# One set of block-diagonal input rows, late modulations side by side, one parameter chain moved to GpSimd, in an adaLN + S4D convolution + token MLP kernel

## The chip, the core and the metric

The kernel runs on one core of a Trainium2 chip. The metric is the device time of one execution in microseconds; the time of a kernel is the median of its runs. The engines are named as in the profile: PE (TensorE), PEld (its weight loads), DVE (VectorE), ACT (ScalarE), POOL (GpSimd) and SP (SyncE, which here only issues DMAs).

## What is computed

The input u has 2048 tokens of 448 channels. Six modulation vectors come from `silu(c) @ w_mod`. They are called 0 to 5 below, in the order of this code. Cut to what matters:

```python
sa, ca, ga, sb, cb, gb = split(silu(c) @ w_mod)       # modulations 0..5, 448 each
h = layernorm(u) * (1 + ca) + sa
# S4D: per channel d a kernel K[d, l] from 256 complex modes, l < 2048
K = 2 * Re(sum_n C[d,n] dt[d] * exp(A[d,n] dt[d] * l))
y = irfft(rfft(h, 4096) * rfft(K, 4096))[:2048] + h * D_skip
x = u + ga * y
h = layernorm(x) * (1 + cb) + sb
out = x + gb * (W2 gelu(W1 h^T + b1) + b2)^T           # along the tokens, F = 1792
```

## The kernel before

Most of the first half is the making of K. The 448 channels are taken in 28 groups of 16, each in two halves, which gives 56 steps, numbered s. For a step PE multiplies small tables with the parameters of its channels (`st_exponents`, `st_phase`: tiles xe and xg in PSUM), ACT takes exponentials and sines, POOL multiplies the magnitudes with the sines (G, two products, L649 and L650) and makes the magnitudes of the upper half (w, m: L628, L630, `st_mag2`), DVE makes E from PSUM (four products, L651 to L655, with two operands of which one is in PSUM), and PE contracts E with G (`st_kgen`, tile kg). Exponentials and sines lie in different table sets of ACT, so the exponentials of eight steps are taken together: `window(s)` at s = 0, 8, 16, ... holds 16 exponentials (L612, tile mag) with their table products, and after it the eight steps have only sines, six ACT instructions each. In a step all engines take their part in an order that is fixed by the code; `flush(dve)` and `flush(act)` put queued closures on those engines. PE, DVE, ACT and POOL each work in program order. The order of the DMAs on SP is set by a scheduler while the pool `first` is open, and is program order from where `first.close()` stands, which is at s = 8.

The parameters of the 448 channels are prepared in four sets of at most 128 channels ("chains", q = 0 to 3). `first_chain` does set 0 ahead of step 0. `chain(q)` does the others a few operations at a time: eight operations on DVE and ACT, then logarithms and exponentials on ACT inside `logs` at the start of window 8, 16 or 24, then 28 more on DVE (tiles of 128 by 256: s, ph, u, xa, p64 and their split into two parts hl, which a DMA on SP stores to `pars`). `WPACE` says how many of these go behind each of the eight exponentials of a window, `pace` how many into each step. `load(g)` reads `pars` back as lex and lph, the operands of the table products.

Beside this runs the input side. `x_load` brings the tokens (tile xt, 16 rows r of 128 tokens by 448), `u_stats` takes mean and variance (L492, L493), `u_scale` the scale and shift, `u_norm` applies them (L508 on ACT, L510 on POOL). Then the first pass of the Fourier transform over the tokens, "rows": `u_rows` multiplies 32-token blocks with the table WU (L523: pu in PSUM), DVE scales by mod[1] on the way out (L526: yt), SP stores yu_d. The second pass, "columns": `u_load` reads yu_d transposed (yi), `u_cols` multiplies with the table S2 (L555), DVE or ACT copies out (L562, L564: uo; DVE where the mod[0] term with the table SV is added), SP stores us_d. The PSUM tiles of rows, columns and modulations come from one pool of three buffers. The rows run in windows 8 and 16 and in steps 8 to 15, the columns in window 24 and in steps 17 to 31. The `modulation` products take the 112 by 448 blocks of w_mod with a broadcast silu(c) (L479: pm, all 128 rows equal), and ACT copies to mod[k] (L483). Number 1, 2 and 3 are made in steps 2 to 7, number 0 at the start of window 8, numbers 4 and 5 at the start of window 16; the last two are loaded into xt.

From step 32 on the products of the two spectra (second channels' half and inverse transform) run under the steps, until about 432 us; then the token MLP: two large products of PE with weights split into two parts by ACT and DVE.

Of the kernel before, what the change touches and what calls it, by code (L numbers as in the profile page):

```python
# [22 lines left out]
P = 128  # L23
# [8 lines left out]
DC = 224  # L32
# [7 lines left out]
def dft_tables():  # L40
# [16 lines left out]
    t["WU"] = np.tile(w1.transpose(1, 2, 0).reshape(32, 64), (4, 1))  # L57
# [45 lines left out]
    t["S2"] = su.reshape(2, 4, 8, 2, 32 * P).transpose(3, 0, 2, 1, 4).reshape(P, 32 * P)  # L103
# [113 lines left out]
def tile_adaln_s4d_mixer(ctx, tc, i, out):  # L217
# [6 lines left out]
    yu_d = dram.tile([2, 32, 2, 8, 4, D], F32, name="yu_d")  # L224
    us_d = dram.tile([2, 32, P, DC], F32, name="us_d")
    v_d = dram.tile([32, P, D], F32, name="v_d")
    x2_d = dram.tile([L, D], F32, name="x2_d")

# [9 lines left out]
    with ExitStack() as es:  # L238
# [27 lines left out]
        def par_load(q):  # L266
            n = min(P, D - P * q)
            raws[q] = {}
            for nm in ("A_C_real", "A_C_imag", "A_log_A_real", "A_A_imag"):
                raws[q][nm] = qp.tile([P, N], F32, tag=nm, name=nm, bufs=2)  # L270
                nc.sync.dma_start(raws[q][nm][0:n], i[nm][P * q : P * q + n])
# [40 lines left out]
        wu = xp.tile([P, 64], F32, name="wu")  # L312
        wms = {}

        def wm_load(k, tile, eng=nc.sync):
            wms[k] = tile
            eng.dma_start(wms[k], i["w_mod"][:, k * D : (k + 1) * D].rearrange("(q p) d -> p q d", p=PP))
# [11 lines left out]
        def wm_slot(k):  # L329
            w = wm0.rearrange("p k d -> p (k d)")[0:PP]  # L330
            return w[:, 4 * D * (k % 4) : 4 * D * (k % 4 + 1)].rearrange("p (q d) -> p q d", q=4)

        late = {
            2: lambda: wm_load(2, wm_slot(2), G),
            3: lambda: wm_load(3, wm_slot(3), G),
            5: lambda: wm_load(0, wm_slot(0), G),
            6: lambda: [
# [3 lines left out]
            9: lambda: nc.sync.dma_start(svt, i["SV"]),  # L343
            10: lambda: [s2_load(0), s2_load(1)],
            11: lambda: [s2_load(2), s2_load(3)],
            12: lambda: wm_load(4, xt[0:PP, 0:4]),
            13: lambda: wm_load(5, xt[0:PP, 4:8]),
# [14 lines left out]

        def chain(q):

# [39 lines left out]
            stt(s, t, -80 * math.log(2.0) / 2.0**80, s, ALU.mult, ALU.add)  # L404
            yield
            stt(s, ya, 0.5, s, ALU.mult, ALU.add)
            yield
            ts(s, s, ldt2[0:n, q : q + 1], None, ALU.add)
# [4 lines left out]
            ts(ph, aim, dt4[0:n, q : q + 1], None, ALU.mult)  # L413
            yield
            ts(u, ph, MAGIC, MAGIC, ALU.add, ALU.subtract)
            yield
            tt(ph, ph, u, ALU.subtract)
# [3 lines left out]
            ts(u, ph, 128.0, MAGIC, ALU.mult, ALU.add)  # L421
            yield
            ts(u, u, MAGIC, None, ALU.subtract)
            yield
            stt(p64, ph, 128.0, u, ALU.mult, ALU.subtract)
# [3 lines left out]
            ts(xa, xa, 4 * i2p, -0.5, ALU.mult, ALU.add)  # L429
            yield  # L430
            ts(u, cr, 0.0, 0.5, ALU.is_ge, ALU.subtract)
            yield
            tt(xa, xa, u, ALU.mult)
            yield
            ts(u, ci, 0.0, 0.5, ALU.is_ge, ALU.subtract)
            yield
            stt(xa, xa, 0.5, u, ALU.add, ALU.mult)
            yield
            stt(xa, ph, 63.0, xa, ALU.mult, ALU.add)
            yield  # L440
            ts(u, xa, MAGIC, MAGIC, ALU.add, ALU.subtract)
            yield
            tt(xa, xa, u, ALU.subtract)
            yield
            yield from split(xa, [(2, 0)])
        def logs(root=False):

            for a, s, u, xa, ya in tmp.values():
                S.activation(u, ya, AF.Square)
                S.activation(s, s, AF.Ln)  # L450
                S.activation(u, u, AF.Ln, bias=1.0)
            if root:
                S.activation(rs, mv[:, :, 1], AF.Ln, bias=eps_t)
# [20 lines left out]
        def modulation(k, *halves):  # L474
# [887 lines left out]
```

## Time and profile before

| | us |
|---|---|
| median of 3 runs | 719.2 |
| lowest and highest run | 718.16 and 723.35 |
| the profiled execution | 723.32 |
| its span | 721.5 |
| mean granted clock of PE | 0.924 of full speed |
| PE, DVE, ACT, POOL busy | 630.4, 453.3, 442.9, 273.4 |

The profiled execution took 1.8 us more than its span, and 4.1 more than the median. A row of a group of instructions has line, engine, operation, the tile written and the tile read with the shapes, the count, busy time and mean time of one in ns, and then the idle time of the engine ahead of those instructions and what ended it. A matmul on 32-bit operands stands as two rows in the trace. The granted clock of PE is 0.50 when the clock is halved and 1.00 at full speed.

### The profile page before, as it was taken

The page shows a single profiled execution, that of the slowest core. Times are in us where ns is not written, and L with a number is a line of the kernel's source. Part 1 is how long each engine was busy: PE and PEld are TensorE (multiplying, and loading weights), DVE is VectorE, ACT ScalarE, POOL GpSimd, SP SyncE. Part 2 cuts the span into 40 slices and gives each one's busy share as a digit, 9 for nine tenths or more (in the row PEclk, how much of TensorE's full clock was granted, in tenths as well). Part 3 has the DMA queues.
Part 4 walks back from the last instruction along what each step waited for, and adds up shares of the span by engine and source line. Part 5 has one row for each costly group of instructions (what it writes and reads, how often), then busy time and mean ns, then how long its engine had stood idle before and what let it go on. Part 6 is the DMA issues. An engine that isn't in the chain of part 4 may idle for free. (4 is left out here: it accounts for less than half of the span.)

```text
span 721.5 us, 18291 instructions
## 1 busy us (share of the span) xinstructions
PE 630.4 (87%) x7204; PEld 455.2 (63%) x7204; DVE 453.3 (63%) x875; ACT 442.9 (61%) x879; POOL 273.4 (38%) x328
## 2 busy tenths in 40 slices
PE   0659989987899888789888949999999999999997
PEld 0334334543544546556565617778999999999996
DVE  7569779769859768476785538778723263334441
ACT  5837588777988889989983549787622242222220
POOL 6487428318729788878884600000000000000000
PEclk9869857787999999989999959999999999999999
DMA  7795464356889645535236979974585436655540
GB/s 168 203 192 139 147 198 138 114 186 164 245 250 254 183 137 131 162 86 152 71 105 184 289 221 257 243 207 112 167 233 153 143 106 176 175 156 153 154 141 25
DMA packets 101636, 121.19 MB, mean 168 GB/s; under 512 B 13067, under 2 KB 87423, under 8 KB 101423
## 3 DMA queue, kind: packets, MB, share of 16 engines
q1 hardware_dynamic: 100014, 113.16, 55.3%
q0 software_dynamic: 1536, 6.87, 4.4%
q8 instruction: 57, 0.93, 0.6%
q14 instruction: 29, 0.23, 0.1%
HBM read 84.64 MB, written 34.87 MB: 166 GB/s over the span
## 5 line engine op out<-in xcount | busy, mean ns | idle before, releaser
L202 ACT CAST whi<-w 128x896 fp32r<-128x896 f32 x64 | 59.7, 938 | 131.4 <-PE o L1329 84.6
L649 POOL TENSOR_TENSOR G<-mag,gs 128x512 f32<-128x512 f32 x56 | 71.9, 1283 | 92.4 <-ACT gs L645 92.4
L211 DVE TENSOR_TENSOR wlo<-w,whi 128x896 fp32r<-128x896 f32 x64 | 68.0, 1087 | 40.3 <-ACT whi L202 27.9
L601 PE MATMUL xg<-tab,lph 64*128 64x512 f32 x112 | 68.0, 609 | 26.6 <-issue 7.9
L1194 PE MATMUL acc<-h3h,whi 128*128 128x448 f32 x224 | 83.5, 373 | 0.1
L1195 PE MATMUL acc<-h3l,whi 128*128 128x448 f32 x224 | 82.0, 366 | 0.0
L1329 PE MATMUL o<-ul,whi 128*128 128x448 f32 x224 | 81.3, 363 | 0.0
L676 PEld LDWEIGHTS kg<-E,G 128*32 128x32 f32 x3584 | 60.7, 121 | 32.5 <-issue 19.4
L1328 PE MATMUL o<-uh,whi 128*128 128x448 f32 x224 | 81.2, 362 | 0.0
L1196 PE MATMUL acc<-h3h,wlo 128*128 128x448 f32 x224 | 81.1, 362 | 0.0
L1330 PE MATMUL o<-uh,wlo 128*128 128x448 f32 x224 | 80.6, 360 | 0.0
L601 PE MATMUL xe<-tab,lph 64*128 64x512 f32 x112 | 66.7, 599 | 12.2 <-ACT gs L646 10.0
L676 PE MATMUL kg<-E,G 128*32 128x64 f32 x3584 | 70.8, 237 | 3.1 <-issue 2.3
L650 POOL TENSOR_TENSOR G<-mag,gs 128x512 f32<-128x512 f32 x56 | 71.7, 1280 | 0.0
L651 DVE TENSOR_TENSOR E<-m,xe 128x512 f32<-128x512 f32 x56 | 38.2, 683 | 39.6 <-ACT xe L644 31.5
L630 POOL TENSOR_TENSOR m<-mag,w 128x512 f32<-128x512 f32 x56 | 59.9, 1069 | 6.0 <-DVE E L655 1.5
L1332 DVE SCALAR_TENSOR_TENSOR y<-o,b,mod 128x448 f32<-128x448 f32 x16 | 10.9, 684 | 80.3 <-PE o L1330 80.3
L642 ACT ACTIVATE ab<-xe 128x512 f32<-128x512 f32 x56 | 33.6, 600 | 31.0 <-PE xe L601 18.4
L1194 PEld LDWEIGHTS acc<-h3h,whi 128*128 128x128 f32 x224 | 42.4, 189 | 13.9 <-ACT h L1250 6.3
L601 PE MATMUL xe<-tab,lex 64*128 64x512 f32 x56 | 31.2, 567 | 19.2 <-DMA lex<-wm 17.4
L601 PEld LDWEIGHTS xg<-tab,lph 64*128 64x128 f32 x112 | 24.0, 214 | 37.1 <-issue 9.8
L612 ACT ACTIVATE mag<-xe 128x512 f32<-128x512 f32 x56 | 35.5, 634 | 17.8 <-PE xg L601 11.1
(231 smaller groups left out, 1485.9 us busy)
## 6 DMA issues: line engine op xcount, KB each, us to landing
w<-in_B_w_dram SPq DMA_DIRECT2D x64, 224.0 KB
w<-in_B_w_dram SPq DMA_DIRECT2D x32, 448.0 KB
yu_d<-yt SPq DMA_DIRECT2D x16, 448.0 KB
yi<-yu_d SPq DMA_DIRECT2D x32, 224.0 KB
us_d<-uo SPq DMA_DIRECT2D x16, 448.0 KB
u<-us_d SPq DMA_DIRECT2D x32, 224.0 KB
v_d<-vt SPq DMA_DIRECT2D x32, 224.0 KB
vt<-v_d SPq DMA_DIRECT2D x16, 448.0 KB
```

The lines of the kernel that those rows point to most:

```text
L211: eng.tensor_tensor(lo, w, hi.bitcast(F32), ALU.subtract)
L601: T.matmul(out[k], lhs[r], rhs[r], start=start, stop=stop)
L630: G.tensor_tensor(m2, me, w[:, :, None].to_broadcast([P, GD, 32]), ALU.mult)
L649: G.tensor_tensor(Gt[:, 1], mg_, v32(sg), ALU.mult)
L650: G.tensor_tensor(Gt[:, 0], mg_, v32(cg_), ALU.mult)
L676: T.matmul(kgs[g][32 * q : 32 * q + 32, m], Gt[:, c, d], E[:, c, d], start=h == 0 and c == 0 and m == 0, stop=h == 1 and c == 1, skip_grou ...
L1194: nc.tensor.matmul(acc[f], hi[:, fs], h3h[:, r], start=r == 0, stop=False)
L1195: nc.tensor.matmul(acc[f], hi[:, fs], h3l[:, r], start=False, stop=False)
L1196: nc.tensor.matmul(acc[f], lo[:, fs], h3h[:, r], start=False, stop=r == 15)
L1328: nc.tensor.matmul(o, hi[:, ks], uh[kh][:, k], start=kh == 0 and k == 0, stop=False)
L1329: nc.tensor.matmul(o, hi[:, ks], ul[kh][:, k], start=False, stop=False)
L1330: nc.tensor.matmul(o, lo[:, ks], uh[kh][:, k], start=False, stop=kh == 1 and k == 6)
```

## The change

It has seven parts.

1. *Rows.* WU becomes block-diagonal: 128 by 128, two blocks of 32 tokens beside each other, so a product takes 64 rows of tokens and gives 128 rows, where it took 32 and gave 64. `u_rows(r)` now does one row of 128 tokens with two products (before: 32 calls with two products each). All 16 rows go into window 8, two behind each of the exponentials 1 to 5 and three behind 6 and 7; of the last ones three rows' products and six yt come in step 8. The layouts of yu_d and S2 follow.
2. *Norms.* Rows 0 to 3 are scaled on DVE, the other twelve on ACT in window 8 (before six on POOL, ten on ACT, eight of these in steps 8 to 15).
3. *Columns.* They begin in step 10 (before in step 17), one or two a step, three each in windows 16 and 24; us_d is stored in 32 pieces of 224 KB instead of 16 of 448 KB. `u_load` begins in step 9 (before 16).
4. *Modulations.* Only 1, 2 and 0 are made early, in steps 2 to 7. Numbers 3 to 5 are made together in steps 19 to 22 by twelve narrow products (32 equal rows each, three side by side in one PSUM tile), copied by ACT as one row each, stored to mod_d in DRAM and read back broadcast. The one that is added to 1 is finished on POOL at step 26. The product of mod[0] and mod[2] moves from DVE in window 8 to POOL in step 8.
5. *Second channels' chain.* The 28 later operations of chain(1) go to POOL, all in window 8, with their six stores on POOL's DMA queue; operations of three inputs become two instructions (`fuse`). The eight earlier ones go from steps 0 to 4 into window 0, and the loads of its parameters onto ACT's queue in `first_chain`. The later operations of the chains 2 and 3 stay on DVE, and lie fully in windows 16 and 24, the earlier ones one per step.
6. *SP.* `first.close()` moves from s = 8 to s = 16, and the SP order up to there becomes program order: the early loads of SV and S2 are issued at steps 9 and 10. The first four rows of u are loaded by SP behind the first lph loads (before by POOL). `u_stats` moves to steps 1 to 7. The loads of a group that begins a new set are issued two steps later.
7. *Tables.* `logs` names the set that holds both logarithm and exponential ahead of its first instruction.

The core of the diff:

```diff
-    t["WU"] = np.tile(w1.transpose(1, 2, 0).reshape(32, 64), (4, 1))
+    wu = np.zeros((2, 2, 32, 32, 2, 2))
+    for g in range(2):
+        wu[:, g, :, :, :, g] = w1.transpose(1, 2, 0)
+    t["WU"] = wu.reshape(P, P)
...
+        def fuse(eng, out, a, c, b, op0, op1):
+            if eng is V:
+                stt(out, a, c, b, op0, op1)
+                return
+            part = a if out is b else out
+            eng.tensor_scalar(part, a, c, None, op0)
+            eng.tensor_tensor(out, part, b, op1)
+
         def chain(q):
+            late_eng = G if q == 1 else V
...
-                V.tensor_copy(hl[:, 0], src)
+                late_eng.tensor_copy(hl[:, 0], src)
                 yield
-                tt(hl[:, 1], src, hl[:, 0].bitcast(F32), ALU.subtract)
+                late_eng.tensor_tensor(hl[:, 1], src, hl[:, 0].bitcast(F32), ALU.subtract)
                 for k, v in places:
-                    nc.sync.dma_start(pars[q][v, k, 0:n], hl.bitcast(F32))
+                    (G if q == 1 else nc.sync).dma_start(pars[q][v, k, 0:n], hl.bitcast(F32))
...
         def logs(root=False):
+            if tmp:
+                S.preload_act_table_set("natural_log_exp_and_others")
             for a, s, u, xa, ya in tmp.values():
                 S.activation(u, ya, AF.Square)
+            if root:
+                S.activation(rs, mv[:, :, 1], AF.Ln, bias=eps_t)
...
+            for k in range(3):
+                r = slice(32 * k, 32 * k + 32)
+                T.matmul(pmods[j][r], scb[:, q, 0:32], wms[j, q][:, k * D : (k + 1) * D], start=q == 0, stop=q == 3)
...
+            def out():
+                S.copy(row[0:96], pm[0:96])
+                nc.sync.dma_start(mod_d[3 * j : 3 * j + 3], row[0:96:32])
+                for k in range(3 * j, 3 * j + 3):
+                    nc.sync.dma_start(mod[k], mod_d[k : k + 1].to_broadcast([P, D]))
...
+        def u_rows(r):
+            R, o = divmod(r, 2)
+            yt = xp.tile([P, 2, D], F32, tag="yt", name="yt", bufs=3)
+            pm = [pms.tile([P, D], F32, tag="ms", name="pu") for _ in range(2)]
+            for g in range(2):
+                p = slice(64 * g, 64 * g + 64)
+                T.matmul(pm[g], wu[p], xt[p, r], start=True, stop=True)
...
+            par_load(1, nc.scalar)
...
-            if s in (8, 16):
-                for k in (0,) if s == 8 else (4, 5):
-                    modulation(k, 0, 1)
...
-                if s in (8, 16):
-                    some(u_rows, rows, (2, 2, 2, 2, 2, 0, 1, 1)[e])
-                elif s == 24 and e != 5:
+                if s == 8 and e == 0:
+                    act.extend([partial(u_norm, 4), partial(u_norm, 5)])
+                elif s == 8:
+                    some(u_rows, rows, 2 if e < 6 else 3)
+                elif s in (16, 24) and e in (2, 4, 7):
                     some(u_cols, cols, 1)
...
-        WPACE = [[0] * 8, [0, 5, 4, 4, 4, 4, 4, 4], [0, 5, 4, 4, 4, 4, 4, 4], [2] * 8]
-        pace = [2] * 32
+        WPACE = [[0, 0, 0, 2, 2, 2, 2, 0], [2, 3, 4, 4, 4, 4, 4, 4], [2, 3, 4, 4, 4, 4, 4, 4], [2, 3, 4, 4, 4, 4, 4, 4]]
+        pace = [0] * 8 + [1] * 24
...
-            if s == 8:
+            if s == 16:
                 first.close()
...
-            if 8 <= s < 16 and free:
-                some(u_rows, rows, 2 if s % 2 else 3)
...
-            if 17 <= s < 32 and free:
-                some(u_cols, cols, 2 if s < 24 else 3)
+            if 10 <= s < 32 and s % BATCH != BATCH - 1:
+                some(u_cols, cols, 2 if free and not 18 < s < 23 else 1)
```

How the instructions then stand shows at three places. First SP's queue in the first chain: svt and s are the tables SV and S2, lex the exponent operands of the first group, which the first exponential needs. Before:

```order
L327 DMA dskr<-in_A_D_skip_dram 1x448 x4
L343 DMA svt<-in_SV_dram 128x17
L540 DMA s_1339<-in_S_dram 128x256
L540 DMA s_1341<-in_S_dram 128x256
L540 DMA s_1425<-in_S_dram 128x256
L540 DMA s_1427<-in_S_dram 128x256
L843 DMA lex_145<-wm_79 32x1x256 x2
L843 DMA lex_146<-wm_79 32x1x256 x2
```

and now:

```order
L332 DMA dskr<-in_A_D_skip_dram 1x448 x4
L874 DMA lex_146<-wm_80 32x1x256 x2
L874 DMA lex_147<-wm_80 32x1x256 x2
L874 DMA lex_148<-wm_80 32x1x256 x2
L874 DMA lex_149<-wm_80 32x1x256
L874 DMA lex_146<-wm_80 32x1x256
L874 DMA lex_149<-wm_80 32x1x256
L874 DMA lex_147<-wm_80 32x1x256
```

The five loads are gone from between dskr and lex.

Second PE's queue in the first part of window 8: pm are modulations, xe and xg the exponents, kg the products of steps 6 and 7, pu the rows of u. Before:

```order
L601 MATMUL xg<-tab,lex_145 128x512
L479 MATMUL pm<-wm_79,scb 128x448 x6
L601 MATMUL xe<-tab,lex_145 128x512
L601 MATMUL xg<-tab,lex_145 128x512
L676 MATMUL kg<-E,G 32x64 x32
L523 MATMUL pu<-xt,wu 64x448 x4
L601 MATMUL xe<-tab,lex_146 128x512
L601 MATMUL xg<-tab,lex_146 128x512
L676 MATMUL kg<-E,G 32x64 x32
L523 MATMUL pu<-xt,wu 64x448 x4
L601 MATMUL xe<-tab,lex_146 128x512
```

and now:

```order
L499 MATMUL pm<-wm_80,scb 128x448 x2
L632 MATMUL xe<-tab,lex_146 128x512
L632 MATMUL xg<-tab,lex_146 128x512
L707 MATMUL kg<-E,G 32x64 x32
L632 MATMUL xe<-tab,lex_147 128x512
L632 MATMUL xg<-tab,lex_147 128x512
L707 MATMUL kg<-E,G 32x64 x32
L555 MATMUL pu<-xt,wu 128x448 x4
L632 MATMUL xe<-tab,lex_147 128x512
L632 MATMUL xg<-tab,lex_147 128x512
L555 MATMUL pu<-xt,wu 128x448 x4
```

The six products of modulations 3 and 0 that stood between two pairs of exponents are two of modulation 0, the row products begin one exponential later, and each writes 128 rows.

Third POOL's queue from the last G of step 7 to the middle of window 8: m and w belong to the magnitudes of the upper halves, xt is the norm of rows of u, and hl, t, s, u and ldt belong to the second channels' chain. Before, with the first G of step 8 at the end:

```order
L650 TENSOR_TENSOR G<-mag,gs 128x512
L510 TENSOR_SCALAR xt<-xt,rs,nm 128x448 x4
L628 TENSOR_TENSOR w<-mag 128x16
L630 TENSOR_TENSOR m_990<-mag,w 128x512
L510 TENSOR_SCALAR xt<-xt,rs,nm 128x448 x2
L628 TENSOR_TENSOR w<-mag 128x16
L630 TENSOR_TENSOR m_1054<-mag,w 128x512
L649 TENSOR_TENSOR G<-mag,gs 128x512
L650 TENSOR_TENSOR G<-mag,gs 128x512
L628 TENSOR_TENSOR w<-mag 128x16
L630 TENSOR_TENSOR m_1292<-mag,w 128x512
```

and now, of which the last row is followed by 29 more of the chain and one more pair of w and m before the first G of step 8 comes:

```order
L680 TENSOR_TENSOR G<-mag,gs 128x512
L681 TENSOR_TENSOR G<-mag,gs 128x512
L391 CAST hl<-A_log_A_real 128x256
L393 TENSOR_TENSOR hl<-A_log_A_real,hl 128x256
L395 DMA pars_58<-hl 128x512 x2
L659 TENSOR_TENSOR w<-mag 128x16
L661 TENSOR_TENSOR m_982<-mag,w 128x512
L375 TENSOR_SCALAR t<-t 128x256
L376 TENSOR_TENSOR s<-t,s 128x256
L375 TENSOR_SCALAR u<-u 128x256
L376 TENSOR_TENSOR s<-u,s 128x256
L425 TENSOR_SCALAR s<-s,ldt_173 128x256
```

The six norms are gone, and the chain with its stores stands between the last G of step 7 and the first of step 8, with the two pairs of w and m inside it.

More of the change, by code (lines that the diff above doesn't have):

```diff
@@ L938, in more @@
                     return
-        rows, cols, pieces = iter(range(32)), iter(range(32)), [0, 0]
+        rows, cols, pieces = iter(range(16)), iter(range(32)), [0, 0]
         def some(f, it, n):
@@ L971, in window @@
             if s == 8:
+                tt(mod[1], mod[1], mod[2], ALU.mult)
                 u_scale()
-                u_norm(0)
-                u_norm(1)
-            if s in (8, 16):
-                for k in (0,) if s == 8 else (4, 5):
-                    modulation(k, 0, 1)
+                for r in range(4):
+                    u_norm(r)
             if s == 0:
@@ L988, in window @@
                 mellow()
-                if s == 8 and e == 0:
-                    tt(mod[1], mod[1], mod[2], ALU.mult)
                 flush(dve)
```

187 lines of the change are left out of this document (92 added, 95 removed).

## The prediction

> **What bounds the kernel now.** I read the busy table of the page first, then a table by stage, then the groups of each stage, then single rows in order of time.
>
> ```profile
> span 721.5 us, 18291 instructions
> PE 630.4 (87%) x7204; PEld 455.2 (63%) x7204; DVE 453.3 (63%) x875; ACT 442.9 (61%) x879; POOL 273.4 (38%) x328
> ```
>
> The 87% of PE is a mean over two different halves. The stages, cut where ACT begins and ends its 16 exponentials of a window, show it:
>
> ```profile
> core 0: us, PE busy (x) PEld busy (x) DVE busy (x) ACT busy (x) POOL busy (x), PEclk, DMA share, GB/s
> 28.30:71.20 42.90, 28.31 (x462) 15.72 (x460) 33.35 (x59) 27.23 (x56) 32.39 (x38) 0.80 0.77 171
> 71.20:99.20 28.00, 26.39 (x272) 11.34 (x273) 21.83 (x54) 16.82 (x33) 9.13 (x12) 0.72 0.55 186
> 99.20:139.80 40.60, 35.32 (x600) 18.25 (x604) 33.83 (x56) 33.53 (x64) 27.80 (x28) 0.73 0.38 130
> 139.80:158.90 19.10, 18.76 (x301) 10.36 (x290) 11.81 (x33) 15.14 (x30) 2.75 (x5) 0.91 0.43 162
> 158.90:193.60 34.70, 28.21 (x472) 14.89 (x475) 32.20 (x54) 29.61 (x60) 27.00 (x28) 0.85 0.74 205
> 193.60:211.40 17.80, 16.22 (x289) 8.90 (x290) 10.72 (x25) 14.32 (x29) 3.84 (x5) 0.90 0.90 243
> 211.40:245.40 34.00, 28.78 (x510) 15.27 (x513) 31.17 (x53) 29.91 (x59) 27.39 (x27) 1.00 0.77 221
> 245.40:257.30 11.90, 11.00 (x264) 7.46 (x255) 5.77 (x12) 9.93 (x19) 9.47 (x16) 0.86 0.74 221
> 432.00:721.50 289.50, 284.76 (x1396) 254.31 (x1395) 142.79 (x286) 115.84 (x197) 0.00 (x0) 0.99 0.60 163
> ```
>
> The rows are, in order: steps 0 to 7, window 8, steps 8 to 15, window 16, steps 16 to 23, window 24, steps 24 to 31, window 32, and the token MLP. In the MLP PE is busy 284.76 of 289.50 us, and the change does not touch it. In windows 8 and 16 PE is nearly full as well (26.39 of 28.00, 18.76 of 19.10) and POOL nearly empty (9.13, 2.75). In the steps no engine is full. Window 32, which has the exponentials and little else, takes 11.90 us; windows 16 and 24 take 7.2 and 5.9 more. So what the change can win is the extra work in the windows and the slack in the steps, all between 0 and 245 us.
>
> What sets the pace of a step is POOL's chain of four operations:
>
> ```profile
> L649 POOL TENSOR_TENSOR G<-mag,gs 128x512 f32<-128x512 f32 x56 | 71.9, 1283 | 92.4 <-ACT gs L645 92.4
> L650 POOL TENSOR_TENSOR G<-mag,gs 128x512 f32<-128x512 f32 x56 | 71.7, 1280 | 0.0
> L630 POOL TENSOR_TENSOR m<-mag,w 128x512 f32<-128x512 f32 x56 | 59.9, 1069 | 6.0 <-DVE E L655 1.5
> L628 POOL TENSOR_TENSOR w<-mag 128x16 f32<-128x16 f32 x56 | 16.1, 287 | 13.7 <-ACT mag L612 13.0 <-DVE yk L720 0.7
> ```
>
> 1.283 + 1.280 + 1.069 + 0.287 = 3.9 us a step, 31.4 for eight. Eight steps last 34.0 to 42.9, so at most 2.6 to 11.5 us can go from a run of eight.
>
> **The change part by part.** The rows that carry its prices are these:
>
> ```profile
> L526 DVE TENSOR_TENSOR yt<-pu,mod 128x448 f32<-128x448 f32 x32 | 18.4, 614 | 10.3 <-PE pu L523 10.3
> L555 PE MATMUL pu<-yi,s 128*128 128x448 f32 x64 | 31.5, 607 | 1.4 <-ACT uo L564 1.3
> L508 ACT ACTIVATE xt<-xt,nm,rs 128x448 f32<-128x448 f32 x10 | 7.1, 766 | 0.0
> ```
> L483 ACT ACTIVATE mod<-pm 128x448 f32<-128x448 f32 x6 | 3.2, 547 | 1.0 <-PE pm L479 0.9
> L999 DVE TENSOR_TENSOR mod<-mod,mod 128x448 f32<-128x448 f32 x1 | 1.5, 1472 | 0.0
> ```
>
> And, of window 16's start and of window 8 alone (the last two rows):
>
> ```profile
> L479 PE MATMUL pm<-xt,scb 112*128 112x448 f32 x16 | 6.3, 546 | 0.0
> ```
> ```profile
> L523 PE MATMUL pu<-xt,wu 32*64 32x448 f32 x46 | 12.2, 819 | 1.6 <-DVE yt L526 0.8 <-POOL xt L510 0.8
> L479 PE MATMUL pm<-wm,scb 112*128 112x448 f32 x12 | 4.8, 548 | 0.0
> ```
> ```profile
> 71.97 1.28 ACT L450 ACT_TABLE_LOAD   x1
> 74.20 1.28 ACT L454 ACT_TABLE_LOAD   x1
> ```
>
> A matmul of the program stands as two in the trace; a row of a timeline begins with its start and its length in us.
>
> *First chain.* SP issues the load of SV and four of S2 ahead of the lex loads, and the first exponential waits 3.85 us for PE, which waits for the lex loads:
>
> ```profile
> 7.46 0.36 SPq L343 DMA_DIRECT2D svt<-in_SV_dram  x1
> 7.91 1.80 SPq L540 DMA_DIRECT2D s<-in_S_dram  x4
> 9.83 9.96 SPq L843 DMA_DIRECT2D lex<-wm  x12
> ```
> ```profile
> 9.43 0.42 ACT L871 ACTIVATE u<-ya 128x256 f32<-128x256 f32 x1 [0.43 <-DVE ya L863]
> 18.23 0.60 ACT L612 ACTIVATE mag<-xe 128x512 f32<-128x512 f32 x1 [3.85 <-PE xe L601]
> ```
>
> Without them SP is 0.36 + 1.80 = 2.2 us earlier. But the four loads of the second channels now stand on ACT's queue ahead of L871. At the 0.45 us each of the S2 row they cost 1.8, less the 0.43 that ACT idles there: 1.4 us later on the chain that the last lex loads come from. 2.2 early on one side, 1.4 late on the other: between -2.2 and +1.4. I take -1.1, since the stage ends with SP's twelve issues (9.96 us), yet only those with data ready can move.
>
> *Steps 0 to 7.* The eight early operations of the second channels leave DVE here for window 0. One of them stood here for 2.55 us, beside two G products that began just ahead of it:
>
> ```profile
> 46.17 0.63 DVE L492 BATCH_NORM_STATS2 st<-xt 128x6 f32<-128x448 f32 x1 [5.56 <-DMA xt<-in_A_u_dram]
> 47.66 2.55 DVE L392 TENSOR_TENSOR ya<-ya,xa 128x256 f32<-128x256 f32 x1
> ```
> ```profile
> 47.43 1.27 POOL L649 TENSOR_TENSOR G<-mag,gs 128x512 f32<-128x512 f32 x1
> 48.66 1.27 POOL L650 TENSOR_TENSOR G<-mag,gs 128x512 f32<-128x512 f32 x1
> ```
>
> Those 2.55 us go. The 5.56 us wait for rows of u stays: steps 1 and 2 still read them, and their loads are issued no earlier. The four moved row statistics add four times 0.6 to DVE here. I take -2.5, the one stall; bounds -7 (stall and wait both go, less the statistics, and the other small operations) and +2 (the statistics alone).
>
> *Window 8.* The modulation matmuls at its start fall from six to two (12 rows to 4: 3.2 us of the 4.8), one of the two table loads of 1.28 us falls out, and DVE loses the 1.47 us product of L999 and the late chain. In its place stand 13 of the 16 rows of u, each two products of 64 rows by 128 columns, and 26 yt. Twenty-six times 0.614 is 16.0 us of DVE against its 21.83 busy before; ACT gets 12 norms instead of 2, 7.7 us more on 16.82, so about 24, less the 1.28. With the start of some 4 us for the logarithms that gives 27: -1.0. Bounds -4 (ACT's 23.2 and nothing else) and +6 (if the pairs of PE and DVE, three PSUM tiles deep, alternate instead of overlapping). The chain that went to POOL is 13 TENSOR_TENSOR, 14 TENSOR_SCALAR, 5 CAST and 6 DMA issues, priced by:
>
> ```profile
> L833 POOL TENSOR_TENSOR wm<-ph,wm 128x256 fp32r<-128x256 f32 x1 | 0.7, 719 | 0.1
> L832 POOL CAST wm<-ph 128x256 fp32r<-128x256 f32 x1 | 0.5, 517 | 2.5 <-DVE ph L891 2.5
> L510 POOL TENSOR_SCALAR xt<-xt,rs,nm 128x448 f32<-128x448 f32 x6 | 5.0, 838 | 4.2 <-DVE nm L501 4.2
> L292 POOL DMA_DIRECT2D xt<-in_A_u_dram x12 | 6.1, 512 | 0.0
> ```
>
> 13 x 0.72 + 14 x 0.53 (0.838 cut toward 256 columns) + 5 x 0.52 + 6 x 0.51 = 22.4 us, and two m in between 2.7: 25. It begins some 5 us in, ends near 30, and the first G of step 8 stands behind it and needs POOL near 27 + 3. The cover is just enough. If it is gone, each us goes to step 8, where POOL has 40.6 - 27.8 us to spare, so the first five cost nothing.
>
> *Steps 8 to 15.* Out go 16 pairs of row products and 16 yt (9.8 us of DVE), and 8 norms of ACT; in come three rows with six yt at the start of step 8 and ten column products in steps 10 to 14. The nearest row is steps 16 to 23, which already hold such column products and a chain: 34.70. To it I add six yt, 3.7, ahead of E in step 8, and take off 1.0 for the chain that runs at half the pace: 37.4, that is -3.2. Bounds -6 (34.7) and 0. The `mod[0]` product on POOL is one operation more there.
>
> *Window 16.* The 16 modulation rows at its start, 6.3 us, go, with eight rows and yt; three column products come, and the chain of third channels, which already ran there. Window 32 is the floor, 11.9; DVE's chain of 28 small operations ran under 11.81 busy us. With the exponentials ACT has 15.14 - 1.28 - 1.1 (two mod copies) = 12.8. I take 13.5: -5.6, bounds -7.2 (11.9) and -3.
>
> *Window 24.* Four column products fewer and a table load fewer, from 17.8 toward the same 13.5: -4.3, bounds -5.9 and -2.
>
> *Steps 16 to 23 and 24 to 31.* Column products move up, leaving some ten and three; four groups of three narrow modulation products come. DVE and ACT work falls by a few us in 34.7 and 34.0, above the floor of 31.4: -1.5 each, bounds -3 and +1 each. The round trip of the last three modulations through DRAM is read only by the MLP at 432 us: nothing. Splitting us_d into twice as many stores is SP's work, hidden under steps in which SP has nothing else due: nothing.
>
> The sum: -1.1 - 2.5 - 1.0 - 3.2 - 5.6 - 4.3 - 3.0 = -20.7. The profiled execution took 723.3 us (span 721.5 and 1.8 around it), 4.1 above the median of 719.2; the sum gives 702.6 for it and 698.5 for the median. I say 699.
>
> **Rivals.** *Half clock in window 8.* In 71.2 to 99.2 the granted clock was 0.72, in steps 8 to 15 0.73, in steps 24 to 31 1.00. If window 8 stays at half, a product of the new kind takes twice the 0.55 of L479's row, twice over as two rows: 2.2; 26 of them, in pairs that run beside each other, are 28.6 us, and the exponentials' and the other products' share (26.39 less 12.2 and 4.8 of the two rows of window 8) 9.4 more: 38 instead of 27, so 699 + 11 = 710. For it: the clock column. Against it: the new products use twice the rows and twice the columns. The other way round, a full clock through window 8 and steps 8 to 15 would take the bounds of both, -4 and -6: 693.
>
> The Trainium skill, page "TensorE: Matmul & The Clock Gate", Part 1, says that the clock is halved by default and full after some 3.4 us of sustained activity, which would make the full clock the case, and 693 the time. The trace does not bear it out as stated: this row has PE busy throughout at half clock.
>
> ```profile
> 94.00:99.20 5.20, 5.20 (x46) 2.01 (x42) 3.54 (x9) 2.09 (x5) 0.00 (x0) 0.50 0.84 306
> ```
>
> *The steps do not get shorter*, because their pace comes from POOL waiting for ACT's sines (92.4 us on L649) and not from what moves: then only the chain and the windows pay: -1.1 - 1.0 - 5.6 - 4.3 = -12, so 707.
>
> *POOL becomes the bound at window 8.* At the price of L630 and L510 without any cut, 13 x 1.07 + 14 x 0.84 + 5 x 0.52 + 6 x 0.51 + 2.7 = 34.1, from 5 on to 39, four beyond what step 8 absorbs; a second four behind it in the steps: 707.
>
> *Slower: column products wait for their input.* They begin at step 10, a few us after the last row is stored, on a PE that works in order, behind an SP that now keeps program order. If each of steps 10 to 14 waits as the statistics waited for u, 5 x 5.56 = 28 us, the time is 726. It decides from 4.2 us a step (20.7 / 5). For it: the DMA share is 0.74 to 0.90 where column products ran. Against it: it is 0.38 in steps 8 to 15, and four buffers are loaded ahead. Two or three such waits give 710 to 715, about no change.
>
> **How the numbers follow.** Forecast 694 to 704: 0.40. Full clock, 693 and under: 0.08. Steps no shorter: 0.14. POOL bound: 0.10. Half clock: 0.10, half of it within 1%. Two or three waits: 0.06. Slower: 0.12. One per cent (7.2 us) is about what a measurement of this kernel can tell from no change. Faster, below 712: 0.40 + 0.08 + 0.14 + 0.10 + 0.05 = 0.77; the same 0.11; slower 0.12. The range 688 to 714 leaves out the slower case, half of the "same" and a little below.
>
> **What would show it.** Right: windows 16 and 24 near 13.5 us, one table load ahead of their exponentials; steps 8 to 15 near 37 with a clock above 0.85; POOL busy for 22 to 25 us of window 8; first exponential near 17. Wrong: the clock at 0.5 through window 8, column products idle on DMA in steps 10 to 14, or G in step 8 waiting on nothing but POOL itself.

## The result, and the profile after

The change makes the kernel slower: 728.14 us median of 4 runs (724.78 to 731.26) against 719.65 (718.16 to 723.35) before, a ratio of 1.0102 with a 95% interval of 1.0064 to 1.0140. The forecast was 699, range 688 to 714. The profiled execution took 731.26 us with a span of 729.5, against 723.32 and 721.5 before.

```profile
span 729.5 us, 18216 instructions
PE 624.8 (86%) x7140; PEld 456.4 (63%) x7140; DVE 447.2 (61%) x851; ACT 438.4 (60%) x876; POOL 294.8 (40%) x357
```

PE, DVE and ACT are busy for less time than before, POOL for 21.4 us more, and the span is 8.0 us longer. So the loss looks like waits, and a table by stage says where. Here the stages are cut at ACT's table loads in the timeline of each kernel (the load for the sines ends a window, the load for logarithms or exponentials begins one), so that they can be compared; they differ a little from the prediction's cuts.

| stage, us | before | after | difference | forecast |
|---|---|---|---|---|
| up to the first exponential | 18.2 | 14.2 | -4.0 | -1.1 |
| window 0 | 8.7 | 9.5 | +0.8 | 0 |
| steps 0 to 7 | 45.0 | 49.6 | +4.5 | -2.5 |
| window 8 | 28.4 | 26.1 | -2.2 | -1.0 |
| steps 8 to 15 | 40.3 | 40.9 | +0.6 | -3.2 |
| window 16 | 19.4 | 13.2 | -6.2 | -5.6 |
| steps 16 to 23 | 34.3 | 51.3 | +17.0 | -1.5 |
| window 24 | 18.2 | 12.7 | -5.4 | -4.3 |
| steps 24 to 31 | 32.9 | 31.4 | -1.5 | -1.5 |
| window 32 | 13.0 | 15.5 | +2.5 | 0 |
| all that follows | 463.1 | 465.1 | +2.0 | 0 |

The same cuts as windows of the trace after, from steps 0 to 7 down to window 32:

```profile
core 0: us, PE busy (x) PEld busy (x) DVE busy (x) ACT busy (x) POOL busy (x), PEclk, DMA share, GB/s
23.70:73.30 49.60, 33.96 (x469) 18.37 (x466) 30.48 (x64) 28.61 (x57) 31.96 (x38) 0.83 0.72 158
73.30:99.40 26.10, 24.48 (x275) 13.18 (x273) 21.47 (x44) 21.57 (x42) 21.25 (x31) 1.00 0.65 254
99.40:140.30 40.90, 33.14 (x573) 19.77 (x574) 33.86 (x51) 29.74 (x60) 38.37 (x42) 0.83 0.74 210
140.30:153.50 13.20, 12.52 (x267) 7.28 (x258) 9.44 (x22) 13.17 (x28) 3.44 (x5) 1.00 0.73 210
153.50:204.80 51.30, 34.27 (x490) 15.91 (x490) 35.92 (x60) 30.19 (x61) 28.30 (x28) 0.77 0.76 212
204.80:217.50 12.70, 11.96 (x286) 7.08 (x284) 10.82 (x26) 12.34 (x25) 2.91 (x4) 1.00 0.54 162
217.50:248.90 31.40, 25.15 (x520) 14.47 (x519) 26.07 (x45) 27.15 (x53) 27.66 (x28) 0.89 0.55 169
248.90:264.40 15.50, 12.91 (x237) 8.30 (x236) 5.86 (x12) 11.02 (x21) 11.48 (x18) 0.78 0.21 54
```

Three things are to be seen. The windows did what was forecast: in window 16 ACT is busy for 13.17 of 13.20 us, the extra work is gone and the window is as short as ACT allows. In steps 8 to 15 POOL is busy for 38.37 of 40.90 us, which makes it the likely bound. In steps 16 to 23 no engine is busy for more than 35.92 of 51.30.

Four waits stand in these steps and just ahead of them. In the timeline a row has start, length, engine, line, operation, tiles, and in brackets the idle time ahead with its releaser. PE first, at the late modulations:

```profile
176.96 0.95 PE L510 MATMUL pm<-wm,scb 112*32 112x448 f32 x6
...
180.93 0.95 PE L510 MATMUL pm<-wm,scb 112*32 112x448 f32 x6
...
190.00 1.72 PE L510 MATMUL pm<-wm,scb 112*32 112x448 f32 x6 [4.14 <-DMA wm<-in_w_mod_dram]
...
199.86 0.95 PE L510 MATMUL pm<-wm,scb 112*32 112x448 f32 x6 [3.78 <-DMA wm<-in_w_mod_dram]
```
```profile
165.63 0.43 SPq L322 DMA_DIRECT2D wm<-in_w_mod_dram  x1
...
172.93 0.42 SPq L322 DMA_DIRECT2D wm<-in_w_mod_dram  x1
...
182.68 0.42 SPq L322 DMA_DIRECT2D wm<-in_w_mod_dram  x1
...
191.94 0.41 SPq L322 DMA_DIRECT2D wm<-in_w_mod_dram  x1
```

The code issues the loads at the start of steps 17, 18, 20 and 21 and uses them in steps 19, 20, 21 and 22. The first two are issued two steps ahead, and their products start without a wait. The last two are issued one step ahead, and the products start 7.3 and 7.9 us after that, where a step of the kernel before is some 4 us (34.3 us for eight). PE works in order, so the whole step stands behind them. Then DVE and ACT, at the end of window 16 and in step 16:

```profile
143.34 0.43 DVE L393 TENSOR_TENSOR hl<-A_log_A_real,hl 128x256 fp32r<-128x256 f32 x1
...
157.09 0.29 DVE L391 CAST hl<-p 128x256 fp32r<-128x256 f32 x1 [7.01 <-DMA pars<-hl]
```
```profile
163.28 0.42 ACT L399 ACTIVATE xa<-A_C_real 64x256 f32<-64x256 f32 x1 [6.44 <-DVE hl L393]
```

The first split of the third channels' chain (its two parts hl) was ready at 143.8 us. Its store went out at 151.76, as SP's queue shows:

```profile
143.71 1.27 SPq L577 DMA_DIRECT2D yi<-yu_d  x2
145.02 0.59 SPq L571 DMA_DIRECT2D s<-in_S_dram  x1
145.72 2.17 SPq L599 DMA_DIRECT2D us_d<-uo  x2
...
151.11 0.54 SPq L622 DMA_DIRECT2D lph<-pars  x1
151.76 2.04 SPq L395 DMA_DIRECT2D pars<-hl  x4
```

Before the change the same store went out as soon as the split was ready:

```profile
150.52 0.42 DVE L376 TENSOR_TENSOR hl<-A_log_A_real,hl 128x256 fp32r<-128x256 f32 x1
```
```profile
150.98 0.84 SPq L378 DMA_DIRECT2D pars<-hl  x2
```

In the changed kernel the loads and stores of the columns, the loads of the last chain's parameters and of lph stood ahead of the store. Which part of the change made this queue so long, the earlier columns, the us_d stores in smaller pieces or the program order of SP, no run takes apart. There are three hl buffers, so the fourth split (L391 at 157.09) waited for the first store to land, and ACT's first operation of the next chain, which takes over the one xa buffer, waited for the last split; ACT's sines and PE stood behind that.

### The profile page after: what moved, and what is told of

Read it like the earlier page. It is cut to its first block, busy times and chain, and to the rows that moved or that the text cites. A ratio compares the mean times of both kernels' runs of the same rounds, so it can differ in the third digit from the quotient of the medians.

```text
span 729.5 us, 18216 instructions
## 1 busy us (share of the span) xinstructions
PE 624.8 (86%) x7140; PEld 456.4 (63%) x7140; DVE 447.2 (61%) x851; ACT 438.4 (60%) x876; POOL 294.8 (40%) x357
## 5 line engine op out<-in xcount | busy, mean ns | idle before, releaser
L214 DVE TENSOR_TENSOR wlo<-w,whi 128x896 fp32r<-128x896 f32 x64 | 68.0, 1087 | 40.3 <-ACT whi L205 31.0
L632 PE MATMUL xe<-tab,lph 64*128 64x512 f32 x112 | 68.3, 612 | 15.9 <-ACT gs L677 7.1
L1358 DVE SCALAR_TENSOR_TENSOR y<-o,b,mod 128x448 f32<-128x448 f32 x16 | 10.9, 682 | 80.3 <-PE o L1356 80.3
L673 ACT ACTIVATE ab<-xe 128x512 f32<-128x512 f32 x56 | 33.8, 603 | 32.1 <-PE xe L632 20.7
L1222 PEld LDWEIGHTS acc<-h3h,wlo 128*128 128x128 f32 x224 | 42.4, 189 | 3.1
L1221 PEld LDWEIGHTS acc<-h3l,whi 128*128 128x128 f32 x224 | 42.6, 190 | 2.6 <-DVE mean L1238 0.4
```

The costliest lines, as they stand in the source:

```text
L214: eng.tensor_tensor(lo, w, hi.bitcast(F32), ALU.subtract)
L632: T.matmul(out[k], lhs[r], rhs[r], start=start, stop=stop)
L1221: nc.tensor.matmul(acc[f], hi[:, fs], h3l[:, r], start=False, stop=False)
L1222: nc.tensor.matmul(acc[f], lo[:, fs], h3h[:, r], start=False, stop=r == 15)
```

## Experiments

In all of them the ratio is to the kernel before, on the same chip. The first four change one place each in the changed kernel (728.1 us).

**Stores of the third channels' chain on GpSimd's queue.**

```diff
-                    (G if q == 1 else nc.sync).dma_start(pars[q][v, k, 0:n], hl.bitcast(F32))
+                    (G if q < 3 else nc.sync).dma_start(pars[q][v, k, 0:n], hl.bitcast(F32))
```

> The changed kernel, with the stores of the third channels' chain in window 16 issued by GpSimd, which is idle there, instead of SyncE. Theory: in steps 16 to 23 (51.4 us after, 34.3 before) a share of the loss is SyncE's backlog: the first split was ready at 143.8 us, its store went out at 151.8, the fourth split waited 7.0 us for its buffer, and ACT's first operation of the next chain 6.4 us for that. Then the waits of 7.0 and 6.4 us are gone or under 1 us, steps 16 to 23 fall by 6 to 8 us, and the time is 719 to 723. Rival: the transfers themselves are slow, since DMA is 0.92 busy there, and an early issue only queues longer; then the wait stays above 4 us and the time is 726 to 729.

Measured: 721.4 us, ratio 1.0030 (1.0005 to 1.0056). The wait of the fourth split is 0.91 us where it was 7.01, and ACT's 6.44 is gone:

```profile
151.21 0.29 DVE L391 CAST hl<-p 128x256 fp32r<-128x256 f32 x1 [0.91 <-DMA pars<-hl]
```

The transfers were not the trouble, SP's order was. Steps 16 to 23 fell only from 51.3 to 48.1 us, 3.3 of the 6.0 us by which the spans differ; another 2.8 lie behind 350 us, where the profiled execution after was the longer one and which the edit does not touch. So this stage bears out about half of what the theory claimed for it while PE's waits for wm, 7.0 us in this run, still stand in it.

**Late modulation products one and two steps later.**

```diff
-            if 18 < s < 23:
-                modulation(1, s - 19)
+            if s in (19, 20, 22, 24):
+                modulation(1, (19, 20, 22, 24).index(s))
...
-            if s == 26:
+            if s == 29:
```

> The changed kernel, with the four groups of late modulation products in steps 19, 20, 22 and 24 instead of 19 to 22, their loads where they were, so that the last two groups have two and three steps between load and use instead of one. Theory: PE's in-order waits for wm (4.1 and 3.8 us at 190 and 199.9 us) come from that single step, the load taking 7 to 8 us; they vanish and the time falls by 6 to 8 us, to 720 to 722. Rival: PE waits there in any case for something else that is late, so that the wait moves to another line and the time falls by less than 2 us, 726 to 729.

Measured: 720.1 us, ratio 1.0009 (0.9974 to 1.0044). The products of steps 19 and 20 stand at 178.48 and 182.46 without a wait, and the trace has none on wm in the two later ones. Steps 16 to 23 took 40.5 us. That is 10.8 us less, of which 4.3 came back in window 24 (17.0 us where it was 12.7). The cause of that is open; with the first edit beside it, below, window 24 took 13.4.

**First four rows of u early again.**

```diff
+            x_load(0, 4, G)
             S.activation(u, ya, AF.Square)
...
-        x_load(0, 4)
```

> The changed kernel, with the first four rows of u loaded by GpSimd in the first chain again, as before the change, instead of by SyncE behind the first lph loads. Theory: steps 0 to 7 (49.6 us after, 45.0 before) lose 12.0 us of DVE to three waits for xt and 7.6 of PE to wm since these bytes were moved from 8.6 us, where nothing waits for them, to 25 us, into a stretch in which DMA is the bound; then the waits for xt shrink by 4 us or more and the time falls by 3 to 6 us, to 722 to 725, though the first exponential, at 14.2 us, may come up to 1 us later. Rival: the early loads delay the lex loads and what is won in steps 0 to 7 is lost in the first chain, 727 to 729.

Measured: 726.8 us, ratio 1.0088 (1.0052 to 1.0125): no difference from the changed kernel that the intervals can tell. Steps 0 to 7 fell by 2.8 us, and the stages ahead of them rose by 2.4. The wait that was left in the steps is PE's:

```profile
59.23 2.61 PE L499 MATMUL pm<-wm,scb 112*128 112x448 f32 x3 [10.49 <-DMA wm<-in_w_mod_dram]
```
```profile
41.00:49.00 8.00, 7.74 (x150) 3.93 (x149) 7.58 (x16) 4.57 (x10) 7.89 (x10) 0.87 0.98 205
49.00:57.00 8.00, 0.00 (x0) 0.00 (x0) 1.40 (x5) 3.95 (x8) 7.58 (x10) 0.77 0.98 192
```

From 41 to 57 us DMA is busy for 0.98 of its time (the last but one column). The weights of modulation 2 land at 59 us whether the steps come there early or late; PE simply waits 10.5 us for them. So the rival holds in the sum: of the 3.2 us by which the steps began earlier in the changed kernel, 2.4 were gained because the rows of u had left the stages ahead, and that was paid back in steps 0 to 7. The first exponential itself hardly moved (14.9 us after 14.2); the second did, which stands at 15.65 us in the changed kernel:

```profile
14.86 0.60 ACT L643 ACTIVATE mag<-xe 128x512 f32<-128x512 f32 x1 [1.02 <-PE xe L632]
18.03 0.60 ACT L643 ACTIVATE mag<-xg 128x512 f32<-128x512 f32 x1 [2.58 <-PE xe L632]
```

**No operation of the next chain in steps 8, 9, 16 and 17.**

```diff
-        pace = [0] * 8 + [1] * 24
+        pace = [0] * 10 + [2, 2, 1, 1, 1, 1] + [0, 0, 2, 2, 1, 1, 1, 1] + [1] * 8
```

> The changed kernel, with no operation of the next chain in steps 8, 9, 16 and 17, and two in steps 10, 11, 18 and 19. Theory: ACT's first operation of the next chain (xa, one buffer) stood 6.6 us in step 8 for the end of the second channels' chain on GpSimd and 6.4 us in step 16 for that on VectorE, and all of ACT's sines behind it; without it steps 8 to 15 fall by 3 to 6 us and steps 16 to 23 by 2 to 6, the time is 718 to 723. Rival: GpSimd itself is the bound of steps 8 to 15 (38.4 of 40.9 us busy), as its chain ends ten us into them, and VectorE's wait stays in step 16; then ACT's wait only changes its name and the time falls by less than 2 us, 726 to 729.

Measured: 728.4 us, ratio 1.0122 (1.0075 to 1.0168). The rival holds. In the changed kernel ACT stood in step 8 at the next chain's first operation:

```profile
109.37 0.42 ACT L399 ACTIVATE xa<-A_C_real 128x256 f32<-128x256 f32 x1 [6.59 <-POOL hl L393]
```

Now ACT gets on with its sines and stands at the third of them, for the buffer of a G that POOL has not made:

```profile
112.23 0.60 ACT L676 ACTIVATE gs<-xg 128x512 f32<-128x512 f32 x1 [2.33 <-POOL G L680]
```
```profile
110.27 0.62 POOL L395 DMA_DIRECT2D pars<-hl  x1 [0.30 <-POOL hl L393]
110.91 1.28 POOL L680 TENSOR_TENSOR G<-mag,gs 128x512 f32<-128x512 f32 x1
```

POOL's chain ends with its last store at 110.9 us, and the first G of step 8 starts only then, 10.6 us behind the end of window 8. Steps 8 to 15 took 41.9 us (40.9 in the changed kernel). DVE's wait in step 16 stayed too (6.36 us for the store of hl), and steps 16 to 23 took 53.7 us (51.3).

**Both mends.** The edits of the first two experiments together.

> The changed kernel with both edits that paid: the stores of the third channels' chain issued by GpSimd, and the late modulation products in steps 19, 20, 22 and 24. If the two losses are separate, their gains add: 6.8 and 8.0 us off 728.1 make 713, with steps 16 to 23 at 36 to 38 us (51.3 after). Rival: both hang on the one backlog of DMA and SyncE in steps 16 to 22 and share their gain, so that the time is 718 to 720.

Measured: 715.2 us, ratio 0.9951 (0.9925 to 0.9977). The gains of some 7 and 8 us add but for some 2 us, which the intervals cannot tell from a full sum. Steps 16 to 23 are 35.2 us, with a larger share of each engine's time in use:

```profile
153.20:188.40 35.20, 29.89 (x486) 14.67 (x486) 32.85 (x52) 29.37 (x59) 27.84 (x30) 0.90 0.88 237
```

That is within 1 us of the value before the change (34.3): 16.1 of the 17.0 us of this stage go with the two edits, more than the 3.3 and 10.8 that they took out singly. PE's granted clock in this stage, 0.85 before and 0.77 after, is 0.90 here, though the edits only move products and stores; so the lower clock went with the waits.

**Second channels' chain on VectorE, or only its last part on GpSimd**, both with the two mends. The lines behind the dots are in the second of the two only.

```diff
-            late_eng = G if q == 1 else V
+            late_eng = V
...
+            if q == 1:
+                late_eng = G
             late_eng.tensor_scalar(xa, xa, 4 * i2p, -0.5, ALU.mult, ALU.add)
```

> As the one with both mends, but the second channels' chain on VectorE in window 8 instead of on GpSimd (its stores stay on GpSimd's queue). Theory: GpSimd's chain runs ten us into step 8 and makes GpSimd the bound of steps 8 to 15 (38.4 of 40.9 us busy); without it steps 8 to 15 fall from 40.9 to 36 to 38 us, while window 8 grows from 26.1 by 3 to 6 us, since VectorE was busy for 21.5 there and 9.7 come on top: within 2 us of the kernel with both mends. Rival: steps 8 to 15 are bound by the six yt and the three rows at the start of step 8 and stay above 40, and the time is 4 us or more above it.

> As the one with both mends, but of the second channels' chain only the last part (xa, 13 of its 38 GpSimd instructions with their store) on GpSimd and the rest on VectorE. Theory: GpSimd is then done near the end of window 8, window 8 is 26 to 28 us, steps 8 to 15 are 37 to 39, and the time is 2 to 4 us below the kernel with both mends, 709 to 711. Rival: GpSimd's part starts so late in the window that it ends as late as before, and the times agree within 1 us.

Measured: 718.5 us, ratio 0.9967 (0.9941 to 0.9993), and 716.7 us, ratio 0.9956 (0.9924 to 0.9989), against 715.2 and 0.9951; the intervals overlap. The first was expected within 2 us of the kernel with both mends, which the intervals neither show nor exclude; the second was expected 2 to 4 us below it, and no gain is to be seen. The stages tell more. With the chain on VectorE, window 8 (first row) and steps 8 to 15 are:

```profile
73.90:105.00 31.10, 25.18 (x275) 13.09 (x273) 29.45 (x71) 21.96 (x41) 6.32 (x10) 1.00 0.57 224
105.00:143.50 38.50, 31.67 (x567) 17.97 (x570) 32.40 (x52) 29.66 (x59) 29.36 (x30) 0.87 0.75 211
```

31.1 + 38.5 = 69.6 us against 26.0 + 40.9 = 66.9 with the chain on POOL. So POOL's chain did lengthen steps 8 to 15 (they fall by 2.4 us without it, to a little above the 36 to 38 expected), but DVE then bounds window 8 (29.45 of 31.10 busy). With only the last part on POOL, steps 8 to 15 were 38.9 us, as expected, but window 8 was 30.9 and not 26 to 28. DVE was busy there for 26.41 us, and POOL's part began only at 95.5 us, 22 us into the window, behind DVE's; it ended at 106.6, 2.6 us into step 8.

**Rows of u in half-width products**, in the changed kernel.

```diff
-                T.matmul(pm[g], wu[p], xt[p, r], start=True, stop=True)
+                for h in range(2):
+                    T.matmul(pm[g][64 * h : 64 * h + 64], wu[p, 64 * h : 64 * h + 64], xt[p, r], start=True, stop=True)
```

> The changed kernel, with each product of the rows of u cut into two that write 64 rows each (the two column halves of the block-diagonal table): the same result by twice the matmuls on tiles half as wide. It tells what made the clock of window 8 go from 0.72 to 1.00. If it is how much of the array a product fills, the clock falls below 0.85 there, window 8 grows from 26.1 to 28 to 31 us and the time to 730 to 734. Rival: it is the regular work without waits, whatever the tile; then the clock stays above 0.95, window 8 within 1 us of 26.1, and the time at 727 to 729.

Measured: 726.8 us, ratio 1.0106 (1.0068 to 1.0144), the time of the changed kernel. Window 8:

```profile
73.60:101.30 27.70, 26.61 (x333) 10.18 (x331) 21.55 (x44) 21.86 (x42) 22.70 (x33) 1.00 0.63 247
```

The clock stays at 1.00, so the width of the products is not what lifted it from 0.72; window 8 is 1.5 us longer for the added products. What did lift it, the 64 rows instead of 32 or something else in the window, is open. Work without gaps was not enough before the change: in the prediction's row from 94.00 to 99.20 us PE was busy for all 5.20 us at 0.50.

**Early modulations 2 and 0 in steps 6 and 7**, with both mends; then **the first rows of u at the end of window 0** on top; then **six of POOL's instructions in another form** on top of that.

```diff
-            if 1 < s < 8:
-                mod_whole((1, 2, 0)[s // 2 - 1], s % 2)
+            for k, h in {2: [(1, 0)], 3: [(1, 1)], 6: [(2, 0), (2, 1)], 7: [(0, 0), (0, 1)]}.get(s, []):
+                mod_whole(k, h)
```
```diff
-        x_load(0, 4)
...
             if s == 0:
+                x_load(0, 4, G)
```
```diff
-            eng.tensor_scalar(part, a, c, None, op0)
+            eng.tensor_scalar(part, a, *((c, 0.0) if op0 == ALU.mult else (1.0, c)), ALU.mult, ALU.add)
...
-            late_eng.tensor_scalar(u, u, MAGIC, None, ALU.subtract)
+            late_eng.tensor_scalar(u, u, 1.0, -MAGIC, ALU.mult, ALU.add)
```

> As the one with both mends (715.2), with the products of modulations 2 and 0 in steps 6 and 7 instead of 4 to 7; modulation 1 stays in steps 2 and 3. Theory: in steps 0 to 7 DMA is the bound (0.98 of its time from 41 to 57 us), the weights of modulation 2 land at 59 us whatever is done, and PE, in order, waits 3.8 to 10.5 us for them with the steps behind it; without the wait steps 0 to 7 fall from 49.4 by 3 to 5 us, and the time to 710 to 712. Rival: the row statistics on VectorE wait for rows that land at 53 to 57 us in the same way and keep the steps as long: less than 1.5 us, 714 to 716.

> As the one before, with the first four rows of u loaded by GpSimd at the end of window 0, some 5 us earlier than by SyncE and after the lex loads. Theory: the first exponential stays near 14.2 us, since nothing is added ahead of the lex loads, and the wait of 5.4 us for xt at the start of step 1 shrinks to under 2; steps 0 to 7 fall by another 2 to 4 us, 707 to 710. Rival: DMA moves the same bytes before the same later rows, and the wait goes to the next rows: within 1 us of the one before.

> As the one before, with six of GpSimd's one-operation TENSOR_SCALAR instructions of the second channels' chain written as a product and a sum (times c, plus 0). The trace has one operation at 0.85 to 0.93 us and product and sum at 0.40 to 0.43, both on 128 by 256. Theory: it is the form that costs, each falls by 0.45, the chain ends 2.5 to 3 us earlier and steps 8 to 15, which start behind it, fall by 1.5 to 3 us. Rival: the longer ones are longer for what stands around them (a lock held by VectorE, a wait); then their times stay above 0.8 and steps 8 to 15 within 0.5 us.

Measured on one chip, on which the kernel before took 723.6 us: 713.1, ratio 0.9880 (0.9805 to 0.9955); 710.9, ratio 0.9830 (0.9767 to 0.9893); 708.7, ratio 0.9811 (0.9756 to 0.9866). The intervals are too wide to tell neighbours apart, so the stages have to. Steps 0 to 7 went from 49.4 us to 48.6, 45.5 and 43.8. The first of the three bears out its rival: the wait for wm at 59.6 us (3.80 us with both mends) is gone, and PE waits for another load that comes as late.

```profile
61.37 0.76 PE L632 MATMUL xg<-tab,lph 64*128 64x512 f32 x1 [6.97 <-DMA lph<-pars]
```

The second bears out its theory, with the first exponential at 13.9 us and a gain of 3.2 us in the steps, though the wait for rows moved to later ones (7.94 us at 44.6 us). In the third the chain's instructions changed as expected, all six to 0.40 or 0.41 us (the shape is the same, only the form differs; one of them is shown):

```profile
L440 POOL TENSOR_SCALAR u<-u 128x256 f32<-128x256 f32 x1 | 0.9, 860 | 0.1
L448 POOL TENSOR_SCALAR u<-A_C_real 128x256 f32<-128x256 f32 x1 | 1.1, 1085 | 0.1
```
```profile
L441 POOL TENSOR_SCALAR u<-u 128x256 f32<-128x256 f32 x1 | 0.4, 404 | 0.1
L449 POOL TENSOR_SCALAR u<-A_C_real 128x256 f32<-128x256 f32 x1 | 1.1, 1082 | 0.1
```

(The first pair is the changed kernel, the second the experiment; L448 and L449 are the same unchanged instruction.) Steps 8 to 15 fell from 41.3 to 38.6 us; in the other runs with the whole chain on POOL they were between 40.7 and 41.9. The 1.7 us by which steps 0 to 7 fell are not the edit's, which changes nothing there. By its ratio this last kernel is faster than both the kernel before and the changed one.

## Why the prediction was wrong, point by point

The sum was -20.7 us, and the spans differ by +8.0. Of the 28.7 us between them, 18.5 lie in steps 16 to 23, 7.0 in steps 0 to 7 and 3.8 in steps 8 to 15; the other stages nearly cancel.

- *Windows 16 and 24, -5.6 and -4.3*: right, -6.2 and -5.4. The extra work was removed, and ACT is the floor.
- *Window 8, -1.0*: right in sign, -2.2. The clock came out at 1.00, which the forecast did not count on. It was the rival with a chance of 0.08, and it held in this window only; in steps 8 to 15 the clock was 0.83. (By its own figures, 23.2 for ACT in a window of 28.0, the lower bound of this term was -4.8 and not -4.)
- *Steps 16 to 23, -1.5*: this is the step that failed, by 18.5 us. It counted the engines' work, found it smaller, and gave the waits for the added loads and behind the added issues no price: "The round trip of the last three modulations through DRAM is read only by the MLP at 432 us: nothing." The round trip did cost nothing (no instruction waits for it in the trace), but what goes into it did: the last two of the four loads of w_mod are issued one step ahead of the products, which PE takes in order, and land 7.3 and 7.9 us later. Moving the products later took out 10.8 us of the stage. Likewise "Splitting us_d into twice as many stores is SP's work, hidden under steps in which SP has nothing else due: nothing." SP did have something due there, the stores of the third channels' chain, which came 8 us late behind the columns' traffic; issuing them elsewhere took out the wait. How much of that the smaller stores made is not shown. Both edits together took out 16.1 us of 17.0.
- *The slower rival* put the waiting in steps 10 to 14, on the columns' own input. There was none there. Its mechanism, an engine in order behind an SP in order behind a crowded DMA, was the right one, in the wrong place and on other transfers: on wm and on pars.
- *Steps 8 to 15, -3.2*: wrong, +0.6. The rival in which POOL becomes the bound came true in its mechanism: the chain ended 10.9 us into the steps, where 3 were expected and five said to cost nothing, and it lasted 33.9 us (76.35 to 110.26), near the rival's 34.1 and not the 25 of the forecast. The slack that was to cover it, 40.6 - 27.8 us, is a total over eight steps; POOL works in order, and the first G of step 8 stood behind the chain. The mis-sized terms are TENSOR_SCALAR, taken at 0.53 us from a row cut to size and measured between 0.40 and 1.09 (twelve of the 14 at 0.85 or more), and the DMA issues, taken at 0.51 and measured at 0.645. Steps 8 to 15 without the chain are 2.4 us shorter, and with six cheaper instructions 2.7; the other 1.1 to 1.4 us of the 3.8 by which this term missed are open.
- *Steps 0 to 7, -2.5*: wrong, +4.5. The 2.55 us stall did go, but the prediction said of the rows' loads that they "are issued no earlier" and left it at that. The first four are issued 16.5 us later (25.1 instead of 8.6 us), into a stretch in which DMA is nearly full (0.95 from 41 to 57 us, and 1.01 before). DVE waited 12.0 us in three places for xt (5.6 in one before), PE 7.6 for wm (1.3 before):

```profile
36.36 0.63 DVE L531 BATCH_NORM_STATS2 st<-xt 128x6 f32<-128x448 f32 x1 [5.18 <-DMA xt<-in_A_u_dram]
...
45.62 0.63 DVE L531 BATCH_NORM_STATS2 st<-xt 128x6 f32<-128x448 f32 x1 [3.85 <-DMA xt<-in_A_u_dram]
```

With the loads back in the first chain these steps were 2.8 us shorter, and with the loads at the end of window 0 they were 3.2 shorter than without; so the rows account for less than half of the 7.0 us by which this term missed, and the rest is open.

- *First chain, -1.1*: right in sign, -4.0, beyond its bound of -2.2. ACT's wait of 3.85 us for PE went whole: SP's lex loads began 1.7 us earlier (8.16 instead of 9.83 us), and their twelve issues took 7.7 us instead of 10.0. With the rows of u back in this stage the issues took 9.5 us again and the start of the steps came 2.4 us later, so more than half of the gain of 3.2 up to there comes from what left the stage and not from the loads of SV and S2. The first exponential was then at 14.9 us, which is within the 13.7 to 15.1 of the other experiments, so most of the 4.0 does not hang on the rows. The loads on ACT cost nothing: its L902 started at 9.36 us (9.43 before), as it waits for DVE in any case.
- *Window 32* was 15.5 us and between 11.7 and 15.6 in the experiments; the cause is open. The +2.0 us of all that follows lies within what the same part took in the experiments, 460.4 to 465.7 us.

## What to carry to other kernels

When a change moves loads, count for each the time from issue to use against the landing time of the same stretch: work that falls on every engine can still end later, because an engine that works in order stops at its first late operand. Here a load took 7.3 to 7.9 us from issue to use, and one step ahead was too late where two steps were enough. A queue in program order needs the same count: list what stands ahead of each store whose buffer somebody waits for. And bytes that are moved out of a stage that waits into one where DMA is already full are not saved, they are lent.

## What was not expected of the hardware

On GpSimd a TENSOR_SCALAR of 128 by 256 took 0.85 to 0.95 us with one operation, 1.07 to 1.09 with a sum and a difference or a comparison and a difference, and 0.40 to 0.43 with a product and a sum; the same value written as a product and a sum took 0.40 instead of 0.86. The clock of PE in window 8 went from 0.72 to 1.00 when the rows came in products of 64 rows, and stayed at 1.00 with half as many columns per product.
